# Token scores of 13 chunks take a way through DRAM instead of a TensorE transpose

## The chip, the core and the metric

The kernel runs on one core of one Trainium2 chip. The metric is the device time of one execution in microseconds, as the median of several executions. A profile of one execution gives the busy time of each engine, the waits and the DMA transfers. Its times run over the span of the profiled instructions, which is about two microseconds shorter than the device time.

TensorE (PE) multiplies and transposes into PSUM, VectorE (DVE) and ScalarE (ACT) read PSUM and SBUF, GpSimd (POOL) works in SBUF, and SyncE (SP) issues DMAs. Each engine executes its own list of instructions.

## The reference

A linear attention with a decaying state (RWKV6) is followed by a mixture-of-depths block. Inputs are r, k, v, w of shape (4, 8, 768, 48): 4 batches, 8 heads, 768 tokens, 48 channels, all float32.

```python
for t in range(S):
    cur = einsum('bhd,bhe->bhde', u[None] * kt, vt)
    y[:, :, t] = einsum('bhd,bhde->bhe', rt, state + cur)
    state = wt[:, :, :, None] * state + einsum('bhd,bhe->bhde', kt, vt)
...
scores = einsum('bsd,d->bs', x, w_gate)      # x: y as (batch, token, 384)
out = x.copy()
for b in range(B):
    top_idx = argpartition(-scores[b], capacity)[:capacity]     # 128 of 768 tokens
    xe = x[b, top_idx]
    ye = maximum(xe @ w1, 0.0) @ w2
    g = 1.0 / (1.0 + exp(-scores[b, top_idx]))
    out[b, top_idx] = x[b, top_idx] + g[:, None] * ye
```

What matters here is the choice of the 128 tokens with the highest scores in each batch. The kernel finds it by ranks: for each token it counts how many tokens of its batch beat it.

## The kernel before

The tokens of a batch are cut into 6 chunks of 128, so that there are 24 chunks in all, numbered 0 to 23 across the batches. A chunk's tokens lie on the 128 partitions. One loop, `turn(i)` (L693), runs from -2 to 24, and in each turn several chunks are worked on at different stages. The order of the instructions on each engine is written out by hand: an engine executes its work in the order in which `turn` names it. For chunk n:

- In turn n - 2 the decays w are transposed on TensorE (`decays_t`, tile ps_w, pool psW with one buffer), and two scans on VectorE make running products from the right and from the left (`scans`, L285 and L296). The k rows are transposed as well (`inputs_t`).
- In turn n - 1 VectorE scales the transposed k and r (`scaled`, L343), and GpSimd forms the products of a token with itself.
- In turn n TensorE makes the attention scores (`scores`, ps_s, L379), VectorE masks them (`masked`, L387), and TensorE makes the outputs (`outputs_t`, L412 and L420) and the update of the state (`carry_products`, L467).
- In turn n + 1 the outputs are turned into rows and stored (`rows_out`, L438), and GpSimd and ScalarE make one score for each token (`row_products`, `row_sums`). They go into a column of the tile `score`, a token on each partition.
- In turn n + 2 the chunk is compared (`compared`, L492).

`compared` needs the scores of a chunk along the free dimension in every partition. TensorE transposes the score column, broadcast to 128 columns, into ps_e, which shares the one psW buffer with the decays (L508). VectorE then compares each token's own score with all earlier chunks of the batch, kept in the tile `every` (L510), and with its own chunk (L514). The results go into `ahead` and are counted in `lost`. ScalarE copies ps_e into `every` for later chunks (L519). When a batch is complete, `mixture` turns the counts into ranks (ps_r, L534), picks the 128 tokens, and gathers their rows by an indirect DMA. `forward` does the two layers of the feed-forward block in small pieces (ps_h and ps_f), which are fed into later turns. This begins with batch 0 in turn 8.

The loads of the inputs are issued by SyncE at the end of each turn (`loads(i + 5)`), two to three turns before they are needed; each moves 192 KB in 1024 rows of 192 bytes. The weights of the feed-forward block are loaded one piece at a time after them, in turns 2, 4 and 6 (w1) and 7 to 10 (w2). SyncE also issues the stores of the output rows (L438). All of these go in one order, that of `turn`, and an instruction that waits for its data holds up those after it.

Two rows are spread over all partitions by a matmul with a row of ones (`spread`, L258): u in turn -1 and the gate weights wg in turn 0. Matmuls on zeros (`warm`, L253) fill the start.

Of the kernel before, what the change touches and what calls it, by code (L numbers as in the profile page):

```python
# [10 lines left out]
FP32 = mybir.dt.float32  # L11
# [6 lines left out]

L = 128
DP = 64  # L20
NBUF = 4
VBUF = NBUF + 1
LOW, HIGH = 0.7, 1.0
# [2 lines left out]
def _rows(ap, n):  # L26

    return dataclasses.replace(ap, ap=[[0, n]] + [list(x) for x in ap.ap])
# [10 lines left out]
def kernel(  # L39
# [40 lines left out]
    nc = tc.nc  # L80
    PSUM = bass.MemoryType.PSUM

    B, H, S, D = r.shape
# [3 lines left out]
    NCH = S // L  # L87
# [4 lines left out]
    W = HP * L  # L92
    DE = DP + D
    assert S % (2 * L) == 0 and C % L == 0 and F % (4 * L) == 0 and H % 2 == 0
    assert HP % 2 == 0 and D <= DP and W <= 512 and C <= 512 and 0 < CAP < S and CAP % L != 1
    assert B * NCH < 256
# [2 lines left out]
    setup = ctx.enter_context(tc.tile_pool(name="setup", bufs=1))  # L99
    lev = ctx.enter_context(tc.tile_pool(name="lev", bufs=2))  # L100
    mod = ctx.enter_context(tc.tile_pool(name="mod", bufs=1))
    psW = ctx.enter_context(tc.tile_pool(name="psW", bufs=1, space=PSUM))
    psT = ctx.enter_context(tc.tile_pool(name="psT", bufs=2, space=PSUM))
    psS = ctx.enter_context(tc.tile_pool(name="psS", bufs=1, space=PSUM))
# [4 lines left out]
    chunks = [(b, ci) for b in range(B) for ci in range(NCH)]  # L109
# [17 lines left out]
    for queue, hs in ((nc.sync, slice(H // 2, H)), (nc.scalar, slice(0, H // 2))):  # L127
        queue.dma_start(
            out=w_bufs[0][:, hs, 0:D], in_=w[0, hs, 0:L, :].rearrange("h t d -> t h d")
# [4 lines left out]
    wg_row = setup.tile([1, C], FP32)  # L134
    nc.scalar.dma_start(out=wg_row, in_=_rows(moe_w_gate, 1))
    u_bc = consts.tile([L, H, D], FP32)
    wg_bc = consts.tile([L, C], FP32)
# [46 lines left out]
    ident = consts.tile([L, L], FP32)  # L184
# [13 lines left out]
    for x in (0, 1):  # L198
        for to, src in ((0, DP * x), (D, DP * (1 - x)), (2 * D, D)):
            n = min(D, DE - to)  # L200
# [12 lines left out]
    for t, sign in ((before_f, 1), (after_f, -1)):  # L213
        nc.gpsimd.memset(t, 1.0)
        nc.gpsimd.affine_select(
            out=t, in_=t, pattern=[[sign, L]], base=-1, channel_multiplier=-sign,
# [28 lines left out]
    score = consts.tile([L, B, NCH], FP32)  # L245
# [3 lines left out]
    def warm(n):  # L249

        ps = psM.tile([L, 512], FP32, tag="m", name="ps_n")
        for _ in range(n):
            nc.tensor.matmul(ps, nothing[:, 0:L], nothing, start=True, stop=True)  # L253

    def spread(to, row):

        ps = psM.tile([L, C], FP32, tag="m", name="ps_b")
        nc.tensor.matmul(ps, one_row, row, start=True, stop=True)  # L258
        nc.scalar.copy(out=to, in_=ps)
# [229 lines left out]

    against = {}  # L490

    def compared(t):  # L492

        b, ci = chunks[t["n"]]
        if ci == 0:
            while len(against) > 1:
                mix()
            against[b] = (
                mod.tile([L, S - L], FP32, name="every", bufs=2),
                mod.tile([L, NCH, S], BF16, name="ahead", bufs=2),  # L500
                lost_bufs[b % 2],
            )
        every, ahead, lost = against[b]
        own = score[:, b, ci:ci + 1]
        lo, hi = ci * L, (ci + 1) * L

        ps = psW.tile([L, L], FP32, tag="w", name="ps_e")
        nc.tensor.transpose(ps, own.to_broadcast([L, L]), ident)  # L508
        if ci > 0:
            nc.vector.tensor_scalar(  # L510
                out=ahead[:, ci, 0:lo], in0=every[:, 0:lo], scalar1=own, scalar2=None,
                op0=ALU.is_ge, op1=ALU.add, accum_out=lost[:, ci, 0:1],
            )
        nc.vector.scalar_tensor_tensor(  # L514
            out=ahead[:, ci, lo:hi], in0=ps, scalar=own, in1=after_f,
            op0=ALU.is_ge, op1=ALU.mult, accum_out=lost[:, ci, 1:2],
        )
        if ci < NCH - 1:
            nc.scalar.copy(out=every[:, lo:hi], in_=ps)  # L519

    def mixture(b):
# [130 lines left out]
    def step(f, n, *more):  # L652
        if 0 <= n < N:
            f(work.setdefault(n, dict(n=n)), *more)

    def mix(n=1, place=None):


        while n > 0 and mixing:
            if place is not None and mixing[0][1] not in (None, place):  # L660
                return
            try:
                mixing[0][1] = next(mixing[0][0])
                n -= 1
            except StopIteration:
                mixing.pop(0)
# [26 lines left out]
    def turn(i):  # L693
        soon = i >= N - 1
        step(first_left, i + 1)
        if i < 1:
            step(scaled_aside, i + 1, "K", "right")
        step(own_products, i + 1)
        step(scores, i)
        step(own_values, i)  # L700
        step(carry, i - 1, work.get(i))
        if i > 0:
            step(scaled, i + 1, "K", "right")
        if i >= 0:
            step(own_weights, i + 1)
        if soon:
            step(masked, i)
        if i == N - 1:
            sums.extend(check_sums())
        if i < N:  # L710
            step(compared, i - 2)
        if not soon:
            step(masked, i)
        step(back, i)
        if i == 0:
            spread(wg_bc, wg_row)
        mix(place="half")
        step(rows_out, i - 1, soon)
        step(row_scores_soon if soon else row_products, i - 1)
        step(own_results, i)  # L720
        fed_in_turn(PIECES // 2, 2 if i >= N - 1 else 1)
        step(inputs_t, i + 1, "R", r_bufs)
        if i == -1:
            warm(1)
        step(scaled, i + 1, "R", "left")
        step(decays_t, i + 2)
        mix(place="mid")
        if i == -2:
            warm(2)
        step(range_check, i + 2)  # L730
        if i == -1:
            spread(u_bc.rearrange("p h d -> p (h d)"), u_row)
            step(own_weights, i + 1)
        step(outputs_t, i)
        step(carry_products, i)
        fed_in_turn(PIECES - PIECES // 2, 1 if i == N - 1 else 0)
        if i == N - 1:
            step(compared, i - 1)
        step(inputs_t, i + 2, "K", k_bufs)
        if i == -2:  # L740
            warm(1)
        if not soon:
            step(row_sums, i - 1)
        step(scans, i + 2)
        if 0 <= i - 2 < N - 1 and chunks[i - 2][1] == NCH - 1:
            mixing.append([mixture(chunks[i - 2][0]), "end"])
        mix(place="end")
        if i > -2:
            loads(i + 5)
        if i in WEIGHT_TURNS:  # L750
            load_weights(1)
# [23 lines left out]
    def general(gen):  # L775
        u_t = gen.tile([D, H], FP32, name="u_t")
        nc.sync.dma_start(out=u_t, in_=u.rearrange("h d -> d h"))
        for b in range(B):
            st = gen.tile([D, H, D], FP32, name="st")
            nc.vector.memset(st, 0.0)  # L780
            with tc.For_i(0, S) as i:
                now = {}
                for name, x in (("r", r), ("k", k), ("w", w)):
                    now[name] = gen.tile([D, H], FP32, name=f"{name}_t")
                    src = x[b, :, bass.ds(i, 1), :].rearrange("h o d -> d (h o)")
                    nc.sync.dma_start(out=now[name], in_=src)
                v_t = gen.tile([D, H, D], FP32, name="v_t")
                src = v[b, :, bass.ds(i, 1), :].rearrange("h o d -> (h o) d")
                nc.sync.dma_start(out=v_t, in_=_rows(src, D))
                kv = gen.tile([D, H, D], FP32, name="kv")  # L790
                nc.vector.tensor_mul(kv, v_t, now["k"].to_broadcast([D, H, D]))
                cur = gen.tile([D, H, D], FP32, name="cur")
                nc.vector.tensor_mul(cur, kv, u_t.to_broadcast([D, H, D]))
                nc.vector.tensor_add(cur, cur, st)
                nc.vector.tensor_mul(cur, cur, now["r"].to_broadcast([D, H, D]))
                nc.vector.tensor_mul(st, st, now["w"].to_broadcast([D, H, D]))
                nc.vector.tensor_add(st, st, kv)
                ps = psM.tile([L, C], FP32, tag="m", name="ps_g")
                nc.tensor.matmul(
                    ps[0:1], ones_f[0:D], cur.rearrange("p h d -> p (h d)"),  # L800
                    start=True, stop=True,
                )
                y_t = gen.tile([1, C], FP32, name="y_t")
                nc.scalar.copy(out=y_t, in_=ps[0:1])
                nc.sync.dma_start(out=out[b, bass.ds(i, 1), :], in_=y_t)
            for c in range(NCH):
                x = lev.tile([L, C], FP32, tag="x", name="x", bufs=3)
                nc.sync.dma_start(out=x, in_=out[b, c * L:(c + 1) * L, :])
                t = dict(n=b * NCH + c, x=x)
                row_scores_soon(t)  # L810
                compared(t)
            for _ in mixture(b):
                pass
            fed(1000)
# [30 lines left out]
```

## Time and profile before

| What | Value |
|---|---|
| Device time, median of 3 | 203.72 us (203.24 to 204.49) |
| Profiled execution, span | 201.8 us |
| Mean granted TensorE clock | 0.996 |
| ps_e transposes (L508) | 24, 318 ns each |
| Copies of ps_e into `every` (L519) | 20, 263 ns each |
| Comparisons with earlier chunks (L510) | 20, 605 ns each |
| Comparisons with the own chunk (L514) | 24, 348 ns each |
| One 192 KB load, issue to landing (median) | 4.5 to 5.4 us |
| Output store, issue to landing (median) | 3.0 us |

Busy times overlap between engines, and a mean over the span hides that the first turns, the middle and the end have different limits. A turn is best recognised in the trace by its score matmuls (ps_s): turn 1 starts at 15.59 us, turn 8 at 58.85, turn 14 at 103.78 and turn 20 at 148.90.

### The profile page before, as it was taken

The numbers are of one execution on the slowest core, as the hardware profiler recorded it, in microseconds if no ns is written. First come the engines' busy times: TensorE is split into PE (matmuls) and PEld (weight loads), VectorE is DVE, ScalarE is ACT, GpSimd is POOL, SyncE is SP. The second block draws the span as 40 slices with busy tenths as digits, with TensorE's granted clock in tenths as the row PEclk, the third lists the DMA queues.
The fourth block names the chain that finished last, engine by engine and source line by source line (L and its number), as shares of the span: only waits on it lengthen the run. The fifth ranks groups of instructions, "written<-read, shape, count | busy, mean of one in ns | idle before, by whom it ended". The sixth has DMA issues, their size and how long they took to land.

```text
span 201.8 us, 6402 instructions
## 1 busy us (share of the span) xinstructions
PE 189.9 (94%) x2290; PEld 153.6 (76%) x2290; DVE 161.2 (80%) x355; ACT 121.0 (60%) x620; POOL 136.7 (68%) x175
## 2 busy tenths in 40 slices
PE   7899999989799899999999999999999999999980
PEld 3478888768687688888887888898887888876940
DVE  6989999999999968988979788988979784961010
ACT  4486877768854775878354865878354866510300
POOL 8497889886857996678538898669538898111202
PEclk9999999999999999999999999999999999999998
DMA  7999999999999999999892994998772221111101
GB/s 115 164 163 153 175 191 206 247 205 216 203 158 255 234 172 217 225 236 180 146 157 59 176 189 105 147 165 151 125 117 68 49 81 44 39 42 42 39 8 44
DMA packets 105387, 28.81 MB, mean 143 GB/s; under 512 B 100482, under 2 KB 104580, under 8 KB 105348
## 3 DMA queue, kind: packets, MB, share of 16 engines
q1 hardware_dynamic: 104304, 26.65, 75.1%
q0 software_dynamic: 512, 1.57, 2.6%
q8 instruction: 20, 0.33, 0.7%
q14 instruction: 19, 0.16, 0.3%
q10 hardware_dynamic: 532, 0.10, 0.3%
HBM read 22.81 MB, written 5.51 MB: 140 GB/s over the span
## 4 chain that ended last, share of the span: by engine, by line
PE 86%; DVE 5%; ACT 2%; POOL 2%; issue 2%; POOLq 0%; DVEq 0%; ACTq 0%
PE ps_s L379 12%; PE ps_h L618 11%; PE ps_f L630 11%; PE ps_yt L412 11%; PE ps_t L265 9%; PE ps_w L265 6%; PE ps_yt L420 5%; PE ps_kv L467 5%; PE ps_y L272 4%; PE ps_t L272 4%; PE ps_e L508 3%; PE ps_n L253 1%; DVE left L296 1%; DVE right_buf L285 1%; PE ps_r L534 1%
## 5 line engine op out<-in xcount | busy, mean ns | idle before, releaser
L364 ACT ACTIVATE rk<-rk 128x48 f32<-128x48 f32 x192 | 43.7, 231 | 0.1
L364 ACT ACTIVATION_READ_ACCUMULATOR rk<-rk 128x1 f32 x192 | 36.3, 189 | 0.0
L437 POOL TENSOR_TENSOR x<-x,vo 128x384 f32<-128x384 f32 x22 | 22.1, 1005 | 19.9 <-ACT x L436 19.8
L425 ACT COPY yt<-ps_yt 128x512 f32<-128x512 f32 x24 | 14.1, 587 | 29.6 <-PE ps_yt L420 27.1
L296 DVE TENSOR_TENSOR_SCAN left<-ps_w,from_left 128x511 f32<-128x511 f32 x24 | 30.7, 1281 | 0.9
L285 DVE TENSOR_TENSOR_SCAN right_buf<-ps_w,from_right 128x511 f32<-128x511 f32 x24 | 29.1, 1211 | 1.1 <-PE ps_w L265 1.1
L387 DVE TENSOR_TENSOR sc<-ps_s,before_f 128x1024 f32<-128x1024 f32 x24 | 29.2, 1219 | 0.8 <-PE ps_s L379 0.8
L379 PE MATMUL ps_s<-R,K 48*128 48x128 f32 x384 | 27.9, 285 | 0.3 <-ACT yt L425 0.2
L412 PE MATMUL ps_yt<-sc,v_buf 128*64 128x128 f32 x384 | 26.3, 278 | 1.6 <-PE ps_w L265 1.4
L379 PEld LDWEIGHTS ps_s<-R,K 48*128 48x128 f32 x384 | 23.3, 187 | 3.9 <-issue 2.9
L618 PE MATMUL ps_h<-xeT,w 128*128 128x128 f32 x192 | 25.6, 280 | 0.2 <-ACT hid L623 0.2
L355 POOL TENSOR_TENSOR rk<-r_buf,k_buf 128x384 f32<-128x384 f32 x24 | 24.2, 1007 | 1.7 <-DMA r_buf<-in_r_dram 1.7
L412 PEld LDWEIGHTS ps_yt<-sc,v_buf 128*64 128x64 f32 x384 | 20.7, 136 | 6.0 <-PE ps_w L265 2.8
L358 POOL TENSOR_TENSOR rk<-rk,u_bc 128x384 f32<-128x384 f32 x24 | 24.1, 1003 | 1.1 <-DVE alls L291 0.5
L618 PEld LDWEIGHTS ps_h<-xeT,w 128*128 128x128 f32 x192 | 22.9, 192 | 1.6 <-ACT xeT L584 0.5
L630 PE MATMUL ps_f<-w,hid 128*128 128x384 f32 x64 | 23.8, 500 | 0.0
L442 POOL TENSOR_TENSOR scr<-x,wg_bc 128x384 f32<-128x384 f32 x22 | 22.0, 1000 | 1.7
L370 POOL TENSOR_TENSOR vo<-v_buf,own 128x384 f32<-128x384 f32 x24 | 19.9, 830 | 1.3 <-ACT rk L364 1.3
L343 DVE TENSOR_TENSOR R<-ps_t,left 128x512 f32<-128x512 f32 x24 | 16.4, 685 | 3.7 <-ACT own L596 1.3
L343 DVE TENSOR_TENSOR K<-ps_t,right_buf 128x512 f32<-128x512 f32 x22 | 15.1, 684 | 4.7 <-PE ps_t L265 4.7
L265 PE MATMUL ps_w<-ident,w_buf 128*128 128x128 f32 x96 | 15.4, 284 | 1.8 <-ACT every L519 1.0
L332 ACT ACTIVATE junk<-w_buf,high 128x384 f32<-128x384 f32 x24 | 15.0, 623 | 0.6 <-DMA w_buf<-in_w_dram 0.6
(112 smaller groups left out, 343.6 us busy)
## 6 DMA issues: line engine op xcount, KB each, us to landing
k_buf<-in_k_dram SPq DMA_DIRECT2D x24, 192.0 KB, 4.5
r_buf<-in_r_dram SPq DMA_DIRECT2D x24, 192.0 KB, 5.4
v_buf<-in_v_dram SPq DMA_DIRECT2D x24, 192.0 KB, 4.7
out_dram<-x SPq DMA_DIRECT2D x24, 192.0 KB, 3.0
w_buf<-in_w_dram SPq DMA_DIRECT2D x23, 192.0 KB, 4.5
w<-in_moe_w_dram SPq DMA_DIRECT2D x3, 512.0 KB, 5.7
w<-in_moe_w_dram SPq DMA_DIRECT2D x4, 384.0 KB, 4.9
w_buf<-in_w_dram ACTq DMA_DIRECT2D x1, 96.0 KB, 3.2
```

Of the source, the lines that this page charges most:

```text
L265: nc.tensor.transpose(ps[:, j, :], src(j), ident)
L285: nc.vector.tensor_tensor_scan(out=flat[:, W - 2::-1], data0=wt[:, W - 1:0:-1], data1=from_right.rearrange("p j t -> p (j t)")[:, W - 2::- ...
L296: nc.vector.tensor_tensor_scan(out=left.rearrange("p j t -> p (j t)")[:, 1:W], data0=wt[:, 0:W - 1], data1=start.rearrange("p j t -> p (j ...
L343: nc.vector.tensor_mul(out, t.pop(name + "t"), t.pop(by))
L355: nc.gpsimd.tensor_mul(rk, r_bufs[n % NBUF][:, :, 0:D], k_bufs[n % NBUF][:, :, 0:D])
L358: nc.gpsimd.tensor_mul(t["rk"], t["rk"], u_bc)
L364: nc.scalar.activation(out=rk[:, h, :], in_=rk[:, h, :], func=AF.Copy, accum_out=o[:, h:h + 1])
L379: nc.tensor.matmul(ps[:, q, j, :], t["K"][rows, j, :], t["R"][rows, j, :], start=True, stop=True,)
L387: nc.vector.tensor_mul(t["sc"].rearrange("p q j t -> p (q j) t"), ps.rearrange("p q j t -> p (q j) t"), _heads(before_f, 2 * HP),)
L412: nc.tensor.matmul(ps[half(c), j % 2, j // 2, :], vt[:, 2 * j + q, :], t["sc"][:, q, j, :], start=(j < 2), stop=(old is None), skip_group_ ...
L618: nc.tensor.matmul(ps[:, q, :], w1[:, dc, (f0 + q) * L:(f0 + q + 1) * L], xeT[:, dc, :], start=(dc == 0), stop=(dc == NDC - 1),)
L630: nc.tensor.matmul(ps, hid[:, fc, :], w2[:, fc, :], start=(fc == 0), stop=(fc == NFC - 1))
```

## The change

For 13 of the 24 chunks (the first five of batches 1 and 2, and the first three of batch 3) the score column no longer goes through TensorE. VectorE transposes it, broadcast to 32 columns, in blocks of 32x32, so that 4 partitions then hold 32 scores each (`scores_out`). SyncE stores these as four packets of 128 bytes to a line in DRAM. At the end of the same turn SyncE reads the line back into all 128 partitions of `every` (`scores_in`), for which the store must have landed. The chunk is compared one turn later than before, in turn n + 3, after r is scaled, and straight from `every`. The ps_e transpose and the ScalarE copy are not needed for these chunks. The other chunks are compared as before, in turn n + 2. So in turn 13 (and in turn 19) the last chunk of a batch is compared early, and the chunk before it later in the same turn.

The purpose is to take work from TensorE and ScalarE and to give up the shared psW buffer. In the same edit the broadcast of the gate weights moves from turn 0 to turn -1, where it replaces a matmul on zeros.

```diff
-    def compared(t):
-
-        b, ci = chunks[t["n"]]
-        if ci == 0:
+    def table(b):
+        if b not in against:
...
+    def by_way_of_dram(n):
+
+        b, ci = chunks[n]
+        return 0 < b < B - 1 and ci < NCH - 1 or 0 < b == B - 1 and ci < NCH - 3
+
+    def scores_out(t):
+        n = t["n"]
+        if by_way_of_dram(n):
+            b, ci = chunks[n]
+            quarters = lev.tile([L, QP], FP32, tag="quarters", name="quarters")
+            nc.vector.transpose(quarters, score[:, b, ci:ci + 1].to_broadcast([L, QP]))
+            t["line"] = lines.tile([L // QP, QP], FP32, name="line")
+            nc.sync.dma_start(out=t["line"], in_=quarters[0:L:QP, :])
+
+    def scores_in(t):
+        n = t["n"]
+        if by_way_of_dram(n):
+            b, ci = chunks[n]
+            every = table(b)[0]
+            nc.sync.dma_start(
+                out=every[:, ci * L:(ci + 1) * L],
+                in_=_rows(t.pop("line").rearrange("q p -> (q p)"), L),
+            )
+
+    def compared(t, late=False):
+
+        if late != by_way_of_dram(t["n"]):
+            return
...
-        ps = psW.tile([L, L], FP32, tag="w", name="ps_e")
-        nc.tensor.transpose(ps, own.to_broadcast([L, L]), ident)
+        if late:
+            ps = every[:, lo:hi]
+        else:
+
+            ps = psW.tile([L, L], FP32, tag="w", name="ps_e")
+            nc.tensor.transpose(ps, own.to_broadcast([L, L]), ident)
...
-        if ci < NCH - 1:
+        if not late and ci < NCH - 1:
             nc.scalar.copy(out=every[:, lo:hi], in_=ps)
...
         if i > 0:
             step(scaled, i + 1, "K", "right")
+        step(scores_out, i - 2)
...
-        if i == 0:
-            spread(wg_bc, wg_row)
         mix(place="half")
...
         if i == -1:
-            warm(1)
+            spread(wg_bc, wg_row)
         step(scaled, i + 1, "R", "left")
+        step(compared, i - 3, True)
...
         mix(place="end")
+        step(scores_in, i - 2)
         if i > -2:
             loads(i + 5)
```

More of the change, by code (lines that the diff above doesn't have):

```diff
@@ L20 @@
 DP = 64
+QP = 32
 NBUF = 4
@@ L101 @@
     mod = ctx.enter_context(tc.tile_pool(name="mod", bufs=1))
+    lines = ctx.enter_context(tc.tile_pool(name="lines", bufs=4, space=bass.MemoryType.DRAM))
     psW = ctx.enter_context(tc.tile_pool(name="psW", bufs=1, space=PSUM))
@@ L502, in compared @@
             )
-        every, ahead, lost = against[b]
+        return against[b]
+    def by_way_of_dram(n):
[21 more added lines that the diff above has]
+            return
+        b, ci = chunks[t["n"]]
+        every, ahead, lost = table(b)
         own = score[:, b, ci:ci + 1]
         lo, hi = ci * L, (ci + 1) * L
-        ps = psW.tile([L, L], FP32, tag="w", name="ps_e")
-        nc.tensor.transpose(ps, own.to_broadcast([L, L]), ident)
+        if late:
[3 more added lines that the diff above has]
+            nc.tensor.transpose(ps, own.to_broadcast([L, L]), ident)
         if ci > 0:
@@ L810, in general @@
                 row_scores_soon(t)
-                compared(t)
+                scores_out(t)
+                scores_in(t)
+                compared(t, by_way_of_dram(t["n"]))
             for _ in mixture(b):
```

## The prediction

> **What bounds the kernel now.** I read the page's busy times and slices first, then busy time by turn, then the chain of waits, and last the order of the SyncE queue, because the change moves work onto that queue.
>
> ```profile
> PE 189.9 (94%) x2290; PEld 153.6 (76%) x2290; DVE 161.2 (80%) x355; ACT 121.0 (60%) x620; POOL 136.7 (68%) x175
> DMA  7999999999999999999892994998772221111101
> ```
>
> TensorE is nearly full over the span, and the DMA engines are full in the first half. The turns differ, as the stretches from one score matmul to the next show (columns: length, PE, PEld, DVE, ACT, POOL busy, clock, DMA share, GB/s):
>
> ```profile
> 27.43:33.40 5.97, 5.86 (x87) 4.95 (x86) 5.87 (x13) 4.60 (x28) 5.19 (x7) 1.00 1.01 199
> 65.49:74.21 8.72, 7.79 (x101) 6.62 (x100) 7.08 (x14) 6.87 (x41) 8.31 (x10) 1.00 1.03 205
> 88.43:95.50 7.07, 7.07 (x81) 5.98 (x80) 6.41 (x12) 5.59 (x31) 5.02 (x7) 1.00 1.04 217
> 126.51:133.54 7.03, 7.03 (x84) 6.04 (x83) 6.36 (x13) 5.63 (x35) 5.51 (x7) 1.00 0.85 140
> ```
>
> Early turns (the first row, turn 3) have PE and DVE both full. From about 74 us PE is the bound and DVE has 0.6 to 0.7 us of slack in 7. The DMA share is still 1.0 at 88 to 95 us and lower later. What one score transpose (ps_e) costs PE is read from the chain, a turn without it (turn 1) against a turn with it (turn 2):
>
> ```profile
> 15.66 1.09 PE ps_s L379 x16
> 16.76 0.53 PE ps_t L272 x4
> ...
> 21.65 1.09 PE ps_s L379 x16
> 22.75 0.25 PE ps_e L508
> 23.00 0.38 PE ps_t L272 x4
> ```
>
> The chain charges 0.25 us to ps_e, but the next transposes then take 0.38 instead of 0.53. The net cost is 0.25 + 0.38 - 0.53 = 0.10 us. Last, the SyncE queue and DVE around turn 9 (turn 9 starts at 65.49):
>
> ```profile
> 65.46 1.12 SPq L180 DMA_DIRECT2D w<-in_moe_w_dram  x1
> 66.67 0.43 SPq L438 DMA_DIRECT2D out_dram<-x  x1
> 67.19 0.38 SPq L148 DMA_DIRECT2D v_buf<-in_v_dram  x1
> ...
> 73.33 0.42 SPq L438 DMA_DIRECT2D out_dram<-x  x1
> ```
>
> ```profile
> 68.85 0.68 DVE L343 TENSOR_TENSOR R<-ps_t,left 128x512 f32<-128x512 f32 x1
> 69.81 1.22 DVE L285 TENSOR_TENSOR_SCAN right_buf<-ps_w,from_right 128x511 f32<-128x511 f32 x1 [0.28 <-PE ps_w L265]
> ...
> 96.21 0.87 DVE L510 TENSOR_SCALAR_CACHE_REDUCE ahead<-every,score 128x640 bf16<-128x640 f32 x1
> ```
>
> The queue issues back to back, and it is late: the weights at 65.46 belong to turn 7, the output rows at 66.67 to turn 8. That out_dram store landed 4.4 us after its issue, because full queues were ahead of it:
>
> ```profile
> DMA to landing us min/median/max: 4.4/4.4/4.4
> ```
>
> At 124 and 130.8 us, with lighter queues, the same store took 2.0 and 2.1 us.
>
> [...]
>
> **The change, part by part.**
>
> Removed: 13 ps_e (chunks 6 to 10, 12 to 16, 18 to 20) at 0.10 us = 1.3 us of PE. In turn 9 PE also waits 0.42 us in front of ps_e and 0.52 us for its psW buffer; at most 0.9 us more. 13 ScalarE copies of 263 ns (L519) go too; ScalarE is busy 60%, so I count nothing.
>
> Moved: the wg_bc broadcast goes from turn 0 to turn -1 in place of a warm-up matmul. In turn -1 PE waits for the first left scan until 7.99, so it is hidden there. In turn 0 it held the R transposes, for which DVE waited 0.40 us; DVE is the binding engine there, so 0.4 us is gained, 0 to 0.5.
>
> Added on DVE: 13 transposes of 128x32 f32. No row shows one; the ends are 0.16 us (the 128x4 product, L291)[...]. I take 0.2, 2.6 us in all, beside PE in turns with 0.6 us of slack, and the compare (0.35 + 0.08 us, plus 0.35 to 0.73 us for earlier chunks) leaves the place ahead of the mask. Nothing on the path.
>
> Added on SyncE, per chunk n: in turn n+2 a store of 4 packets (wait for DVE), the output rows, then a read into all partitions that waits for the store's landing, then the four loads. Behind that wait stand k, r, v, w and weights for later turns. DVE waits for the read in turn n+3, after R, and behind that DVE instruction stand both scans, the next K and the next mask; PE waits for K and the mask. For the last chunk of a batch (chunk 11 in turn 13, 17 in 19) the wait is worse: its early compare reads 640 columns of `every`, including the previous chunk's line, ahead of the mask of the same turn.
>
> First read: the store for chunk 6 takes the place of out_dram at 66.67, lands at 66.67 + 4.4 = 71.1; the read is issued then, and the loads start at 71.6 instead of 67.19. The read lands 1.8 us after issue (out_dram took 2.0 with light queues, and this is smaller; ends 1.5 and 2.5), so 72.9. DVE wants it at 69.5, after R at 68.85 + 0.68: a stall of 3.4 us in turn 9.
>
> Then the queue's cycle, from one v load to the next. While SyncE waits, the DMA engines run dry. With a dry start, v issued at 110.38 to w landed (113.02 + 4.1 = 117.1) is 6.75 us. With second-layer weights add 1.0 us: the queue's period in the trace is 6.4 us with them (66.67 to 73.33 to 79.28 to 86.00 to 92.41) and 5.4 without (24.65 to 29.93, 35.85 to 41.29). The store behind them adds 0.3 and the read's issue 0.5: 8.55 us with weights (turns 8, 9, 10), 7.55 without (turn 11), against PE turns of 7.0 to 7.2. So the lag grows: v loads at 71.6, 80.2, 88.7, 97.3, 104.8. The read for chunk 10 goes out 0.5 before the last of these, 104.3, and lands at 106.1. DVE began chunk 11's early compare at 96.21. Now 106.1 + 1.4 (compare) + 1.2 (mask) = 108.7 before PE can go on with the outputs of turn 13, which started at about 99.25: 9.4 us late. The earlier stalls lie within this, as they are on the same chain.
>
> Later: after turn 13, which has no pair, the queue is no longer ahead of time but near PE. A cycle of 7.55 against turns of 7.5, 7.2, 7.0, 7.1 (turns 15 to 18), and a read wanted more than a turn after its store: about 2 to 3 us are left in turns 15 to 18, and about 0 for chunk 17's early compare in turn 19. Chunks 18 to 20 meet almost no loads. Inputs: k of chunk 12, issued at 67.66, was wanted at about 80; a shift of 4.4 fits, and PE is late itself after that.
>
> Sum: 203.7 + 9.4 - 0.8 (eight ps_e after turn 13; the earlier savings disappear in the stall) = 212.3. The store uses four packets[...]; 0.3 us less in each of five cycles is 1.5. I take 211.
>
> **Rivals.**
>
> 1. Hidden: the line lands in about 2 us even under load. Then the cycle is about 3.8 (five issues) + 0.1 + 2.1 + 0.5 = 6.5 us, as now, and no lag grows. For it: four packets are tiny, and light queues gave 2.0. Against it: out_dram from the same queue position took 4.4. Time: 203.7 - 1.3 - 0.9 - 0.4 = 201.1, and a few tenths from ScalarE: 200.9. This is the one on the other side.
>
> 2. Partial: cycles of 7.5 and 7.0[...]. From 70.6: 70.6 + 3 x 7.5 + 7.0 = 100.1, the read lands at 101.4, DVE is 5.2 us late; less 0.8 and what DVE's slack takes, 207.
>
> 3. Worse: chunk 17's compare waits too (1 to 2 us), and loads held behind the waits arrive late once more: 216.
>
> **How the numbers follow.** Forecast 0.62, hidden 0.12, partial 0.17, worse 0.09. Hidden is faster by over 1% except for a small part (0.11). Within 1% (201.7 to 205.8) are that part and the lower end of partial: 0.10. Slower: 0.79. The range leaves out hidden and the top of worse: 203.5 to 216.
>
> **What would show it.** Right: SyncE gaps ahead of the read of `every`, released by its own store, of 3 to 4.5 us in turns 8 to 12; DVE waits on that DMA in turns 9 to 13, the longest before chunk 11's compare; a DMA share below 1 at 70 to 105 us; turn 14 starting 8 to 10 us later than 103.78. Wrong: the store landing in 2 us at 67 us, DVE finding `every` ready in turn 9, or turns 9 to 13 no longer than before.

## The result, and the profile after

The changed kernel takes 222.87 us (median of 4 runs, 219.97 to 224.4), against 203.69 us for the kernel before. The ratio is 1.0889, with a 95% interval of 1.0777 to 1.1002. It is slower, as forecast, but by 19.2 us where 7.3 were forecast. The medians are over all executions of a run, but the ratios leave out executions over 1.5% above the fastest of the same kernel (here the one of 224.4 us), and the profiles of e2, e6 and e11 are of such executions. The profile after is of the fastest of the four runs (span 218.1 us), so that it explains 16.3 of the 19.2 us, and the text comes back to the rest.

The page first: busy time, DMA in 40 slices, and the shares of the chain that ended last. In the kernel before, TensorE had 86% of that chain.

```profile
PE 194.6 (89%) x2276; PEld 156.4 (72%) x2276; DVE 163.5 (75%) x368; ACT 119.5 (55%) x607; POOL 136.9 (63%) x175
DMA  8999999999998859689693297799690321111101
PE 52%; DMA 22%; DVE 14%; SPq 6%; issue 3%; ACT 1%; POOL 0%; POOLq 0%; DVEq 0%; ACTq 0%
```

TensorE has less to do (2276 matmuls instead of 2290) and is yet busy for 4.7 us longer, a first hint that some of its work ran at a lower clock (the mean granted clock is 0.965, before 0.996). The DMA engines, which were full in the first half before, now have holes from the thirteenth slice on (65 us). And 22% of the chain are transfers.

The stretches from one score matmul to the next (columns: length; PE, PEld, DVE, ACT, POOL busy; clock, DMA share, GB/s) show where the time is. They are turns 9, 10, 12, 13, 17 and 19, and below them turn 13 of the kernel before:

```profile
65.42:73.97 8.55, 7.61 (x100) 6.51 (x99) 3.57 (x7) 5.44 (x27) 8.28 (x10) 1.00 0.77 179
73.97:84.70 10.73, 8.91 (x97) 7.45 (x97) 8.47 (x19) 4.97 (x26) 5.79 (x7) 0.84 0.87 158
91.70:99.91 8.21, 7.25 (x79) 5.91 (x78) 6.20 (x13) 5.04 (x25) 4.64 (x5) 1.00 0.79 160
99.91:116.28 16.37, 11.64 (x113) 8.76 (x113) 10.51 (x23) 6.56 (x41) 4.85 (x6) 0.79 1.08 165
138.79:145.56 6.77, 6.77 (x84) 5.96 (x83) 6.45 (x16) 5.48 (x34) 5.29 (x7) 1.00 0.90 149
152.52:165.00 12.48, 10.02 (x114) 7.80 (x113) 8.30 (x18) 5.89 (x39) 4.41 (x5) 0.86 0.84 141
```

```profile
95.50:103.78 8.28, 8.28 (x113) 6.66 (x112) 6.50 (x13) 5.09 (x32) 4.55 (x5) 1.00 0.94 158
```

Turns 10, 12, 13 and 19 are long. With the same stretches of the kernel before, the whole difference of the two profiles can be added up:

| Stretch | Before, us | After, us | Difference |
|---|---|---|---|
| up to turn 9 | 65.49 | 65.42 | -0.1 |
| turns 9 and 10 | 15.90 | 19.28 | +3.4 |
| turns 11 and 12 | 14.10 | 15.21 | +1.1 |
| turn 13 | 8.29 | 16.37 | +8.1 |
| turns 14 to 18 | 36.84 | 36.23 | -0.6 |
| turn 19 | 8.29 | 12.48 | +4.2 |
| turns 20 to 22 | 21.16 | 20.94 | -0.2 |
| after turn 22 | 31.76 | 32.11 | +0.4 |

The waits point to a cause, which the experiments then test. These are the two compare lines of VectorE (L548 against the own chunk, L544 against earlier ones) and SyncE's wait ahead of the read (columns: total us, times, longest):

```profile
DVE ahead L548 <- DMA every<-line: 10.7, 4, 5.0
DVE ahead L544 <- DMA every<-line: 6.6, 2, 3.9
```

```profile
SPq L524 <- DMA line<-quarters: 17.2, 8, 2.7
```

The SyncE queue around turn 9, and the last pair of that batch. The store of the line took the place of the output store at 66.67 us in the kernel before:

```profile
66.43 0.64 SPq L517 DMA_DIRECT2D line<-quarters  x1
...
70.05 0.33 SPq L524 DMA_DIRECT2D every<-line  x1
70.47 0.39 SPq L150 DMA_DIRECT2D v_buf<-in_v_dram  x1
...
100.74 0.76 SPq L517 DMA_DIRECT2D line<-quarters  x1
...
104.54 0.33 SPq L524 DMA_DIRECT2D every<-line  x1
```

The read follows its store by 3.62 us (70.05 - 66.43) and by 3.80 us (104.54 - 100.74). SyncE issues the output store in between and then stands still, for 2.3 to 2.7 us in these five pairs. VectorE's side, with the idle time ahead of an instruction and its releaser in brackets:

```profile
67.03 0.21 DVE L515 STREAM_TRANSPOSE quarters<-score 128x32 f32<-128x32 f32 x1
...
73.90 0.75 DVE L548 SCALAR_TENSOR_TENSOR ahead<-every,score,after_f 128x128 bf16<-128x128 f32 x1 [4.95 <-DMA every<-line]
...
107.75 0.88 DVE L544 TENSOR_SCALAR_CACHE_REDUCE ahead<-every,score 128x640 bf16<-128x640 f32 x1 [3.87 <-DMA every<-line]
...
156.87 0.88 DVE L544 TENSOR_SCALAR_CACHE_REDUCE ahead<-every,score 128x640 bf16<-128x640 f32 x1 [2.70 <-DMA every<-line]
```

The compare at 107.75 is the one that began at 96.21 before. From the issue of its read it is 3.21 us (107.75 - 104.54); for the five reads of this batch it is 3.85, 3.29, 3.14, 2.91 and 3.21 us. The chain of waits in turn 13 (start, us, what) goes from read to store to read, through VectorE to TensorE:

```profile
96.58 2.89 DMA every<-line
...
100.74 3.78 DMA line<-quarters
...
104.54 3.10 DMA every<-line
...
110.15 1.72 PE ps_yt L414 x16
111.87 1.03 PE ps_yt L422 x16
```

Sixteen matmuls of L422 take 1.03 us here and 0.58 in an undisturbed turn. Cut finer, the stretch shows that the granted clock is at half just behind each of TensorE's two waits in this turn (the waits first, in brackets):

```profile
103.18 0.29 PE L542 MATMUL ps_e<-ident,score 128*128 128x128 f32 x1 [2.11 <-DVE left L298]
...
108.97 0.66 PE L267 MATMUL ps_w<-ident,w_buf 128*128 128x128 f32 x4 [2.10 <-DVE ahead L548]
```

```profile
105.00:107.00 2.00, 1.86 (x6) 0.89 (x4) 0.00 (x0) 0.82 (x3) 1.63 (x2) 0.50 0.35 70
107.00:109.00 2.00, 0.04 (x1) 0.04 (x1) 1.25 (x5) 0.00 (x0) 2.00 (x3) 0.99 1.16 202
...
111.00:113.00 2.00, 2.00 (x29) 1.31 (x26) 1.93 (x7) 0.00 (x0) 0.00 (x0) 0.50 1.17 240
```

### The profile page after: what moved, and what is told of

Read it like the earlier page. It is cut to its first block, busy times and chain, and to the rows that moved or that the text cites. A ratio compares the mean times of both kernels' runs of the same rounds, so it can differ in the third digit from the quotient of the medians.

```text
span 218.1 us, 6398 instructions
## 1 busy us (share of the span) xinstructions
PE 194.6 (89%) x2276; PEld 156.4 (72%) x2276; DVE 163.5 (75%) x368; ACT 119.5 (55%) x607; POOL 136.9 (63%) x175
## 4 chain that ended last, share of the span: by engine, by line
PE 52%; DMA 22%; DVE 14%; SPq 6%; issue 3%; ACT 1%; POOL 0%; POOLq 0%; DVEq 0%; ACTq 0%
DMA line<-quarters 10%; DMA every<-line 9%; PE ps_f L664 8%; PE ps_s L381 7%; PE ps_yt L414 7%; PE ps_h L652 7%; SPq L150 6%; PE ps_t L267 5%; PE ps_yt L422 4%; DVE right_buf L287 3%; DMA k_buf<-in_k_dram 3%; PE ps_kv L469 3%; PE ps_w L267 3%; PE ps_t L274 3%; PE ps_y L274 3%
## 5 line engine op out<-in xcount | busy, mean ns | idle before, releaser
L439 POOL TENSOR_TENSOR x<-x,vo 128x384 f32<-128x384 f32 x22 | 22.1, 1003 | 19.4 <-ACT x L438 19.2
L414 PE MATMUL ps_yt<-sc,v_buf 128*64 128x128 f32 x384 | 28.6, 295 | 2.8 <-PE ps_w L267 1.9
L414 PEld LDWEIGHTS ps_yt<-sc,v_buf 128*64 128x64 f32 x384 | 22.6, 145 | 7.7 <-PE ps_w L267 3.6
L664 PE MATMUL ps_f<-w,hid 128*128 128x384 f32 x64 | 24.5, 511 | 0.0
L485 POOL TENSOR_TENSOR state<-mid,alls 128x192 f32<-128x192 f32 x16 | 8.1, 509 | 25.8 <-PE ps_t L274 16.6
L267 PE MATMUL ps_t<-ident,r_buf 128*128 128x128 f32 x96 | 15.1, 280 | 2.9 <-DVE K L345 2.5
```

The lines of the kernel that those rows point to most:

```text
L267: nc.tensor.transpose(ps[:, j, :], src(j), ident)
L414: nc.tensor.matmul(ps[half(c), j % 2, j // 2, :], vt[:, 2 * j + q, :], t["sc"][:, q, j, :], start=(j < 2), stop=(old is None), skip_group_ ...
L439: nc.gpsimd.tensor_add(xj, xj, vo)
L664: nc.tensor.matmul(ps, hid[:, fc, :], w2[:, fc, :], start=(fc == 0), stop=(fc == NFC - 1))
```

## The experiments

The theory after this profile: VectorE waits for the read, and that wait, passed on through the store and the queue from chunk to chunk, makes the time; the read takes nearly twice the 1.8 us forecast. The rivals: it is SyncE's standing still that matters, as the loads behind it come late; or the extra bytes on full DMA engines; or the order of the two compares in turns 13 and 19; or the moved spread.

### The spread alone (e5)

The kernel before, with only the broadcast of the gate weights moved:

```diff
-        if i == 0:
-            spread(wg_bc, wg_row)
...
         if i == -1:
-            warm(1)
+            spread(wg_bc, wg_row)
```

> The kernel before with one part of the change alone: the gate weights are spread in turn -1 in place of a matmul on zeros, and not in turn 0. The prediction gave it 0.4 us (0 to 0.5): 203.3 us. If VectorE and the DMA engines set the pace of the first turns, none of it is left: 203.7 us.

Measured: 203.55 us (13 runs, 203.41 to 203.72), ratio 0.9993 (0.9985 to 1.0001). The move by itself is worth at most 0.3 us and most likely nothing. The 0.4 us that the prediction gave it are not there.

### Is it the wait on the read? (e1)

All stores, reads and SyncE's waits stay. Only the destination of the read changes, and the compares take their numbers from a weight tile:

```diff
-                out=every[:, ci * L:(ci + 1) * L],
+                out=sink[:, ci * L:(ci + 1) * L],
...
         if late:
-            ps = every[:, lo:hi]
+            ps = w1[:, 0, lo:hi]
```

> The changed kernel with every instruction and transfer of it kept, but the read goes into a tile of its own that nobody uses, and from batch 1 on the comparisons take a resident weight tile instead of every; the rows gathered and scattered are fixed ones (the first 128 of a batch). Left out: the true comparison, so other rows are mixed. Theory A (SyncE waits for the store, so the read comes late, and VectorE waits for the read): VectorE never waits, SyncE still does; the input loads come up to 12 us later but have that slack, so 201 to 204 us. Rival B (the added packets in full DMA engines and the late loads cost the time): 215 us or more. Rival C (the added VectorE work and its new place cost it): 215 us or more.

Measured: 205.45 us (16 runs, 203.86 to 208.78), ratio 1.0081 (1.0063 to 1.0098). Of the 19.2 us, 17.4 are gone. The trace shows that SyncE does what it did in the changed kernel. The first and the last read of the first batch go out at nearly the same times (70.05 and 104.54 there):

```profile
68.79 0.33 SPq L529 DMA_DIRECT2D sink<-line  x1
...
104.82 0.33 SPq L529 DMA_DIRECT2D sink<-line  x1
```

So a SyncE that stands still, loads that are issued up to 12 us late and the added transfers together cost under 2 us (a little more than expected). The loads have that much slack. The rest of the time is lost only where VectorE needs the read.

### What does the read itself cost? (e2, e3)

Both leave out the dependence on the store: the source is a weight array in DRAM that nobody writes. In e2 all partitions read the same 512 bytes, as in the changed kernel; in e3 each partition reads another row.

```diff
-                in_=_rows(t.pop("line").rearrange("q p -> (q p)"), L),
+                in_=_rows(moe_w1[0, 0:L], L),      # e2
+                in_=moe_w1[0:L, 0:L],              # e3
```

> The changed kernel, but the read takes 512 bytes of a weight row from DRAM instead of the score line, so SyncE need not wait for the store; VectorE still waits for the read. Same packets and bytes, one source row read 128 times. The rows mixed are fixed ones, and the scores compared are not the true ones. Theory A: the queue's cycle is 7.3 us with weights and 6.2 without, so the lag doesn't grow; the read lies behind the queued loads and lands 4 to 5 us after issue, a stall of about 3 us in turn 9 and of 3 to 4 at the compare of chunk 11: 205 to 209 us. Rivals B and C: as after, 218 us or more.

> As e2_read_no_wait, but the read takes 128 different rows of 512 bytes of the weights. If 128 reads of the same 512 bytes are what makes the read land 3 to 4 us after its issue, instead of the 1.8 us of the prediction, the reads land 1 to 2 us sooner and the time is 1 to 2 us below e2_read_no_wait; if any read of 128 small packets takes that long, the same within 0.5 us.

Measured: e2 206.98 us in one run and 210.43 to 210.74 in three (median 210.49), e3 204.42 us (18 runs, 203.1 to 205.77), ratio 1.005 (1.0032 to 1.0067). The same 64 KB, issued at the same place, thus cost at least 2.6 us more when they come from one row, and 6 in three of the four runs. VectorE's waits in the two, e2 first (in a run of 210.54 us):

```profile
DVE ahead L552 <- DMA every<-in_moe_w_dram: 7.2, 3, 3.4
DVE ahead L548 <- DMA every<-in_moe_w_dram: 2.3, 2, 2.1
```

```profile
DVE ahead L552 <- DMA every<-in_moe_w_dram: 0.6, 1, 0.6
```

In e2 the five reads of the first batch go out 7.45 us apart on average (68.16 to 97.94), in e3 6.55 (65.84 to 92.03). In these two profiles a cycle of the queue with a read of one row is thus about 0.9 us longer than one with a read of 128 rows. The median landing of all 13 reads is about the same, 3.5 us in e2 and 3.6 in e3. From issue to compare the first read takes 3.97 us in e2 (68.16 to 72.13) and 3.46 in e3 (65.84 to 69.30), both issued close behind loads.

In e3 SyncE never waits for a line and VectorE hardly for a read, and the kernel is still 0.9 us slower than the kernel before. Together with e1 this shows that neither wait alone makes the loss. SyncE's wait for the store costs under 2 us where nobody needs the read (e1). VectorE's need for the read costs 0.9 us where SyncE doesn't wait (e3), or 3.4 and more from one row (e2). The changed kernel has both, one behind the other, and loses 19.

In e1, e2, e3 and e13 the rows gathered are fixed ones. The stretch after turn 22 is 32.0 us in e1, e3 and e13 and 32.1 in the changed kernel, so this hardly matters.

### One batch at a time (e6, e7, e8, e10)

The changed kernel with the way by DRAM for one batch alone; e10 is e8 with the spread left where it was:

```diff
-        return 0 < b < B - 1 and ci < NCH - 1 or 0 < b == B - 1 and ci < NCH - 3
+        return b == 1 and ci < NCH - 1      # e6
+        return b == 2 and ci < NCH - 1      # e7
+        return b == 3 and ci < NCH - 3      # e8, e10
```

> The changed kernel with the way through DRAM for chunks 6 to 10 alone (batch 1). Theory A: these are the turns in which the DMA engines are full, the lag grows to the compare of chunk 11, and turn 14 starts 12 us late as in the changed kernel: 214 to 217 us. If the cost went by the number of packets or of VectorE instructions (5 of 13 chunks): 211 us.

> The way through DRAM for chunks 12 to 16 alone (batch 2). Theory A: one stall of about 4 us, at the early compare of chunk 17 in turn 19, and nothing in turns 15 to 18: 206 to 208 us. By the number of packets or instructions: 211 us.

> The way through DRAM for chunks 18 to 20 alone (batch 3), where hardly any load is queued. Theory A: no stall; three transposes less at 0.1 us: 203.0 to 203.7 us. By the number of packets or instructions (3 of 13): 208 us.

> The way through DRAM for chunks 18 to 20 alone, with the broadcast of the gate weights left in turn 0 and the matmul on zeros in turn -1, as before the change. With the broadcast moved, the same three chunks gave 204.6 us with executions from 203.75 to 206.53, and the profiled one had TensorE at half clock from 10 to 14 us, a stage in which the way through DRAM does nothing yet. If the missing matmul lets the clock drop, this kernel is steady and at 203.0 to 203.6 us; if the scatter belongs to the way through DRAM, it stays at 204 to 206.

| Run | Chunks by DRAM | Median, us | Ratio (95%) |
|---|---|---|---|
| e6 | 6 to 10 | 217.77 | 1.0608 (1.0553 to 1.0663) |
| e7 | 12 to 16 | 208.19 | 1.0242 (1.0227 to 1.0256) |
| e8 | 18 to 20 | 204.59 | 1.0053 (1.0032 to 1.0074) |
| e10 | 18 to 20, old spread | 204.08 | 1.0023 (1.0013 to 1.0032) |

By the ratios the differences from before are 12.4 + 4.9 + 1.1 = 18.4 us, for 18.1 of the whole change, so that the batches hardly interact. The first one, under the full DMA queues (a DMA share of 1.03 over turns 9 to 12 of the kernel before), makes two thirds of it. Even the last one, with light queues (0.20 over turns 20 to 22), gains nothing. The 9 runs of e10 lie within 0.5 us of one another and the 18 of e8 within 2.8 (203.75 to 206.53), and the 13 of e5, with the moved spread and no way by DRAM, within 0.3. This scatter thus comes with the two together.

### The order of the compares (e4)

In turns 13 and 19 the last chunk's early compare, which reads the line just loaded, and the late one before it move behind the scans:

```diff
-        if i < N:
+        if i < N and i - 2 not in (11, 17):
             step(compared, i - 2)
...
-        step(compared, i - 3, True)
+        if i - 2 not in (11, 17):
+            step(compared, i - 3, True)
...
         step(scans, i + 2)
+        if i - 2 in (11, 17):
+            step(compared, i - 3, True)
+            step(compared, i - 2)
```

> The changed kernel, but in turns 13 and 19 the comparisons of the last chunk of the batch and of the one before come after both scans of the turn instead of ahead of the mask. Theory A: the wait for the read then holds neither mask nor scaled r nor scans; turn 13 gains about 3.3 us and turn 19 about 2.5, 216 to 218 us. Rivals B and C: nothing changes, 220 to 224 us.

Measured: 213.78 us (4 runs, 213.59 to 215.29), ratio 1.0515 (1.0472 to 1.0559). This is 9.1 us less than the changed kernel. Turn 13 takes 10.86 us instead of 16.37, turn 19 9.32 instead of 12.48; turn 20 gets longer, 9.71 instead of 8.04. The waits of turns 9 to 12 stay:

```profile
DVE ahead L548 <- DMA every<-line: 12.0, 4, 4.4
```

So nearly half of the loss comes from the place of these compares, ahead of the mask and the scans, which is more than was expected. Of the rest, 5.3 us are in turns 10 to 12, which take 26.55 us instead of 21.28 before.

### The pair on ScalarE's queue (e9)

Store and read are issued by ScalarE, a separate queue in the trace (q10: 2508 packets, 532 in the changed kernel), and SyncE never waits for them:

```diff
-            nc.sync.dma_start(out=t["line"], in_=quarters[0:L:QP, :])
+            nc.scalar.dma_start(out=t["line"], in_=t.pop("quarters")[0:L:QP, :])
...
-            nc.sync.dma_start(
+            nc.scalar.dma_start(
                 out=every[:, ci * L:(ci + 1) * L],
```

> The changed kernel with the store and the read of the score line issued by ScalarE instead of SyncE (the store after the copy of kt, the read at the end of the turn). All 13 chunks, same transfers; the lines no longer lie behind the input loads in the same queue, and SyncE waits for nothing new. Theory A: the store lands in about 2 us and the read is out by the end of the turn, no growing lag; what is left is a short wait at the early compares of chunks 11 and 17 (2 to 4 us each) and some issue time on ScalarE: 205 to 211 us. If the DMA engines' work itself (13 reads of one line) sets the time wherever it is issued: 216 us or more.

Measured: 209.38 us (4 runs, 208.63 to 211.81), ratio 1.0261 (1.0243 to 1.0279). Of the 19.2 us, 13.5 are gone. The read lands no faster (3.9 us, median, from issue to landing), but VectorE waits 4.7 us for it in all instead of 17.3: the five reads of the first batch go out at 67.32 to 95.75 us, up to 9 us earlier than behind the loads of SyncE. Turns 9 and 13 are still 11.41 and 10.02 us long.

### Two ways to give the line more time (e11, e12)

e11 compares two turns later than the kernel before, reads after the loads, and takes one chunk less of each batch by DRAM (11 in all). e12 keeps the order of the changed kernel and takes only chunks 12 to 15 and 18 to 20, where the queues are lighter. Both leave the spread as before.

```diff
+        return 0 < b < B - 1 and ci < NCH - 2 or 0 < b == B - 1 and ci < NCH - 3      # e11
-        step(compared, i - 3, True)
+        step(compared, i - 4, True)                                                   # e11
+        return b == 2 and ci < NCH - 2 or b == 3 and ci < NCH - 3                     # e12
```

> Broadcast as before the change; SyncE issues the read after the loads of the turn instead of ahead of them, the comparison comes one turn later still (n + 4), and the last two chunks of batches 1 and 2 stay on TensorE (11 chunks through DRAM). Theory A: the store has landed when SyncE comes to the read, so the loads are held up by nothing, and VectorE finds the line or nearly so: 202.0 to 203.5 us. If the repeated read of one line costs about 2 us of the DMA engines each, batch 1 still shows one stall of 2 to 4 us: 205 to 207 us.

> Broadcast as before the change; the way through DRAM only where the trace shows slack: chunks 12 to 15 and 18 to 20, so that no early compare needs a line that is still on its way. Theory A: no wait at all and seven transposes less at 0.1 to 0.28 us: 202.6 to 203.3 us, the fastest here. If every chunk on this way costs something by itself: 204 us or more.

Measured: e11 218.51 us (6 runs), ratio 1.0711 (1.0674 to 1.0748); e12 206.69 us (6 runs), ratio 1.016 (1.0132 to 1.0188). Both missed a point of the code: the first chunk of a batch that still goes through TensorE is compared early, ahead of the mask, and needs the line of the chunk before it, which is then on its way. In e11 this is chunk 10 in turn 12, which takes 17.26 us, and chunk 16 in turn 18, which takes 12.81. In e12 it is chunk 16 in turn 18, which takes 9.80 us and where VectorE waits 3.2 us. The wait in e11:

```profile
DVE ahead L544 <- DMA every<-line: 8.3, 2, 8.0
```

### How much of it is the one row? (e13)

The changed kernel with every wait kept, but the line is stored to the first of 128 rows in DRAM, and each partition reads another row:

```diff
-            t["line"] = lines.tile([L // QP, QP], FP32, name="line")
-            nc.sync.dma_start(out=t["line"], in_=quarters[0:L:QP, :])
+            t["line"] = line_bufs[n % 4]
+            nc.sync.dma_start(
+                out=t["line"][0].rearrange("(q p) -> q p", p=QP), in_=quarters[0:L:QP, :]
+            )
...
-                in_=_rows(t.pop("line").rearrange("q p -> (q p)"), L),
+                in_=t.pop("line"),
```

> The changed kernel, with every wait kept, but the read takes 128 different rows of 512 B: the line of four packets is stored into row 0 of a tile of 128 rows in DRAM, the other rows were filled in turns 1 to 4, and all partitions but the first therefore compare with something other than the chunk's scores. The rows that are mixed are taken as a fixed list, so that the work behind the compare stays the same. It leaves out the true comparison. If most of the excess over the forecast is that 128 partitions read the same 512 bytes of DRAM (2 us a read in the loaded stretch between the two earlier kernels that read without a wait), the wait on the line shrinks in turns 9 to 13 and the time is 213 to 216. If the store and the order of the SyncE queue carry it, the time stays at 221 to 224.

Measured: 215.18 us (4 runs, 213.98 to 216.67), ratio 1.0558 (1.0491 to 1.0624). The interval lies wholly below that of the changed kernel. The read for chunk 10 goes out later than there, and VectorE still starts earlier; the last line is the same compare in turn 19, which no longer waits for the read:

```profile
105.26 0.33 SPq L531 DMA_DIRECT2D every<-line  x1
```

```profile
107.11 0.88 DVE L551 TENSOR_SCALAR_CACHE_REDUCE ahead<-every,score 128x640 bf16<-128x640 f32 x1 [2.23 <-DMA every<-line]
...
154.31 0.88 DVE L551 TENSOR_SCALAR_CACHE_REDUCE ahead<-every,score 128x640 bf16<-128x640 f32 x1 [0.86 <-ACT kt L404]
```

From issue to compare it is 2.40, 1.76, 1.88, 1.74 and 1.85 us for the five reads of the first batch, where the changed kernel has 2.91 to 3.85. Turn 19 takes 9.56 us instead of 12.48, which is 2.9 of the 3.7 us between the two profiles. Turns 9 to 13 together take 50.4 us instead of 50.9. There the run has a handicap: its four stores of 64 KB that fill the other rows go through SyncE's queue in turns 1 to 4, and its first line is stored at 68.93 us instead of 66.43. What the faster read would gain in these turns without that delay, no run shows.

### How much of it is TensorE's clock? (e14)

Ten matmuls of zeros before ps_e and ten before the decays, in turns 13 and 19:

```diff
+        if i in (13, 19):
+            warm_y(10)
         if i < N:
             step(compared, i - 2)
...
+        if i in (13, 19):
+            warm_y(10)
         step(decays_t, i + 2)
```

> The changed kernel, with ten matmuls of zeros before the last compare's score and ten before the decays in turns 13 and 19, where TensorE stands for the compare. If the granted clock that falls after those waits is a part of the excess, turn 13 gets shorter by 1 to 1.5 us and turn 19 by 0.5 to 1, and the time is 220 to 221.5. If the clock doesn't follow TensorE's idle time there, or the wait is what counts alone, the time is 222 to 225.

Measured: 219.98 us (4 runs, 219.54 to 221.05), ratio 1.0799 (1.0777 to 1.0821). The intervals overlap, so the times alone decide nothing. The stretches of turns 11, 13 and 19 say more:

```profile
83.20:96.36 13.16, 9.81 (x84) 8.37 (x83) 8.38 (x21) 4.94 (x28) 6.69 (x8) 0.74 0.74 155
...
103.33:117.37 14.04, 12.69 (x132) 8.57 (x132) 10.19 (x21) 6.11 (x38) 4.54 (x5) 1.00 1.04 167
...
153.61:166.17 12.56, 12.40 (x132) 8.65 (x133) 8.43 (x18) 5.89 (x39) 4.42 (x5) 1.00 0.87 151
```

The clock stays at 1.00 in turns 13 and 19, in which TensorE is busy for 12.69 of 14.04 and for 12.40 of 12.56 us. It falls to 0.74 in turn 11, where nothing was added and TensorE stands idle for 3.35 of 13.16 us. In these three turns, then, the clock went with TensorE's idle time. From the start of the compare to the next turn it is 6.99 us in turn 13 (117.37 - 110.38), against 8.53 without the matmuls. In turn 19 it is 7.63 against 8.13. Turn 19 as a whole isn't shorter, as its read went out later.

### The start (e15)

The changed kernel with the spread where it was before:

```diff
+        if i == 0:
+            spread(wg_bc, wg_row)
...
         if i == -1:
-            spread(wg_bc, wg_row)
+            warm(1)
```

> The changed kernel with the spread of the gate's row left where it was, before the turns. If the runs of the changed kernel lie apart from one another by over 4 us because of the start (a clock dip in turn 0 that was seen in kernels with both the moved spread and the way by DRAM), the runs come to lie within 1.5 us of one another at 219.5 to 221. If the start has no part in it, 222 to 224 with the same scatter.

Measured: 221.51 us (4 runs, 220.48 to 223.62), ratio 1.0864 (1.0822 to 1.0907). The runs still lie 3.1 us apart, so the start doesn't explain most of the scatter. It has a part in other runs: in the profiles of e6 and e8, both with the moved spread, the granted clock is 0.50 and 0.51 from 12 to 14 us, and turn 0 takes 7.76 and 6.16 us. In the changed kernel it takes 5.53, and with the old spread at most 5.81. The profiled run here is the longest one. Its turn 14 begins at 119.34 us, 3.1 later than in the profile of the changed kernel: there the first read goes out at 71.49 instead of 70.05, and the compare that ends the chain begins at 110.12 instead of 107.75. In this one run, then, the excess arose in the chain of reads in turns 9 to 13. What varies there from run to run wasn't found.

## Why the prediction was right and wrong

**The transposes removed.** Predicted 0.10 us of TensorE for each, 0.8 after turn 13. Right: turns 14 to 18 and 20 to 22 are 0.6 + 0.2 = 0.8 us shorter. Turn 17 gained 0.28, turns 14 and 20 nothing: the sum is what was predicted, but a single transpose does not cost the same in every turn.

**The spread.** Predicted a gain of 0.4 us; e5 shows none that can be told from zero. Turn 1 begins at 15.59 us in e5 as before, so the wait of VectorE that it took away didn't set the end of turn 0.

**The VectorE transpose.** Predicted 0.2 us; the trace has 0.21 at 67.03. Right.

**The store's landing.** Predicted 4.4 us, 0.3 less for its four packets (the author's estimate, tested by no run). The read went out 3.3 to 3.8 us after the store. The prediction also let the wait hold up the loads behind it, and the trace shows this: SyncE waits for lines for 17.2 us in all, and the v load that goes out at 67.19 in the kernel before goes out at 70.47.

**The queue's cycle.** Predicted reads at 71.1 and 104.3 us; measured 70.05 and 104.54. The cycle was 8.62 us on average ((104.54 - 70.05) / 4), predicted 8.3. The queue was forecast well, but in part by luck, with two small errors against each other: the store landed earlier, and the issues between read and next store took longer (5.2 to 5.7 us with weights, 70.05 to 75.71 in the first cycle, where 8.55 - 4.4 = 4.2 was counted). The 1.5 us taken off at the end for an earlier landing of the store were therefore not there: the longer issues had used them up.

**The read's landing, the step that failed.** The prediction said "The read lands 1.8 us after issue", from an output store under light queues, with 2.5 as the upper end. It took 2.9 to 3.9 us. The output store gave the right number for the wrong thing: it goes to different rows. With 128 different rows the same read took 1.7 to 2.4 us (e13). That one row costs more than 128 also where nothing was freshly written, e2 against e3 shows (at least 2.6 us of the kernel's time, though not of the median landing). Whether the freshness of the line adds to the landing, and why reads of one row are slow, no run shows. This step is worth about 4.3 us of the 9.0 by which the profile exceeds the forecast: 1.4 in turn 13 and 2.9 in turn 19. With a read that lands as forecast the kernel takes 215.18 us (e13), within the range but 4 us above the forecast, so that the terms below failed too.

**After the compare.** Predicted 7.1 us from compare to turn 14 (106.1 to 103.78 + 9.4 = 113.2), measured 8.53. Kept busy, TensorE needs 6.99 (e14). The missing term is the clock: it was granted at 0.50 at 105 and at 111 us, each time behind a wait of TensorE of 2.1 us. The prediction counted waits of TensorE but not what they do to the work behind them.

**Turn 13, added up.** Turn 14 was predicted at 111.7 (113.2 less the 1.5) and came at 116.28, 4.6 us later: 1.7 because the last read went out at 104.54 and not at 102.8, 1.4 because it took 3.2 and not 1.8, and 1.4 for the clock.

**Turn 19.** The prediction left a slack of "about 0 for chunk 17's early compare in turn 19", and put no stall into the sum; the turn grew by 4.2 us. In the third rival this wait was named, at 1 to 2 us. The read went out 0.7 us into the turn (153.22), and its landing decides: with different rows the turn is 2.9 us shorter (e13), and the low clock is worth about 0.5 (e14).

**The rest.** These two make 4.6 + 4.2 = 8.8 of the 9.0 us between the forecast (a span of about 209.1) and the profile. The further 2.9 us to the median are a scatter that the kernel before doesn't have (1.3 us over its four runs) and that the range hadn't allowed for.

**What was to be seen.** SyncE's gaps, the DMA share below 1 in turns 9 to 12 and VectorE's waits in turns 9 to 13 came where they were forecast. Three details differ: SyncE's gaps ahead of the read were 2.3 to 2.7 us, not 3 to 4.5, as it issues the output store meanwhile; the longest wait was the first (4.95 us), not that before chunk 11's compare (3.87), and turn 14 came 12.5 us later, not 8 to 10.

**The rivals.** "Hidden", 200.9 us, did not come about even with no wait for the line: e3 has 204.42. In e3's profile turns 8 to 12 win 0.9 us, and turns 13 and 19, in which VectorE has the compares of two chunks, lose 0.6 and 0.3 again. None of the versions run was measurably faster than the kernel before.

## What to carry to other kernels

When a value goes through DRAM, count three times and not one: the store's landing on the queue that waits for it (here 3.3 to 3.8 us from store to read), the read's landing on the engine that needs it (2.9 to 3.9), and what that engine holds up. Here neither wait cost much alone (under 2 us in e1, 0.9 in e3), but one behind the other, under full queues, they cost most of 19 us. Take the price of a transfer from one with the same access pattern: here 128 reads of one row, behind the wait for the store, took 2.9 to 3.9 us, and 128 reads of 128 rows 1.7 to 2.4 (e13). And move a consumer behind the work that others wait for before touching how it gets its data: that alone was worth 9 of 19 us (e4). Issuing the pair from ScalarE, away from the loads, was worth 13.5 (e9).

## What the runs showed of the hardware

- One row of 512 bytes in DRAM read into 128 partitions landed 2.9 to 3.9 us after issue, with 128 different rows 1.7 to 2.4 us, both issued after SyncE had waited for the store (changed kernel and e13, first batch). Without that wait too, every run with 13 reads of one row (206.98 to 210.74 us, e2) was longer than every run with 13 reads of 128 rows (203.1 to 205.77 us, e3), with a median landing of 3.5 and 3.6 us.
- Loads that go out up to 12 us later than planned cost under 2 us here (e1).
- The granted clock of TensorE fell to half (0.50) after each of two waits of 2.1 us, 5.8 us apart in turn 13. With TensorE kept busy it stayed at 1.00, and the work behind the second wait took 6.99 us instead of 8.53 (e14).
